# Four small VectorE operations per unit: two of them placed behind the first maximum of a step

## The chip, the core and the metric

The kernel runs on one core of one Trainium2 chip. The metric is the device time of one execution in microseconds (us). A run gives the time of several executions; one further execution is recorded by the hardware profiler, and every row shown below comes from that one.

## What is computed

The reference is one block of a transformer with a gate, for 2048 rows of 512 numbers, all in float32:

```python
xn = _layernorm(x)
# attention, 32 heads of 16, one shared key and value head
q = (xn @ wq) in 32 heads;  k = xn @ wk;  v = xn @ wv
p = softmax(q @ k.T * 16 ** -0.5)
s = (p @ v, heads side by side) @ wo
# two dense layers with Mish between them, then SiLU
h = xn @ w1 + b1
g = silu((h * tanh(softplus(h))) @ w2)
return x + s * g
```

The softmax needs the maximum of every row of scores. The kernel computes the scores twice: once to find the maxima, once (transposed) to take the exponential, with the negated maximum already added inside the matmul.

## The kernel before, in words

**Units and steps.** The queries are cut into 32 units: 4 chunks of 512 rows by 8 groups of 4 heads. A unit takes 16 steps, so there are NS = 512 steps; one step takes about 2.85 us. The loop at L1477 writes out, step by step, the instructions of all engines. Every engine then works through its own list in order and waits only on semaphores. In a usual step stand:

- four score matmuls `m` (L1059) whose results go to three PSUM banks (pool `ps_m`, L130), and behind each one a VectorE maximum over its 512 columns (`top`, L1062 to L1063, tile `mb`). They run 20 steps (LEAD) ahead of the exponentials;
- four score matmuls `e` (L1039) and behind each a ScalarE exponential into `pt` (L1041);
- a share of the dense layers, called filler: matmuls into one PSUM bank `xps` (L118), a group of 9, 12 or 15 at a time, written as two halves of 64 rows each, half by half in two steps. The halves are mixed with the `m` and `e` work by `waves` (L637). Some groups end with a VectorE operation that reads the bank (`y`, L851 or L920), and the next group can start only behind it. To let that operation go early, `waves` holds back the last maxima of such a step (L667, L673);
- at the end of the step the product with the values, `pv` (L1116). Its eight rows per step are a good mark of where TensorE is.

**The four operations.** When all maxima of a unit are there, `c_rows` (L1078) turns them into two rows for each pair of heads. `reduce` (L1085) takes the maximum over the four key blocks; `parts` writes the negated maximum in the reduced matmul format (L1088) and what that format loses (L1090); `turn` (L1095) transposes the result into a tile `cr`, of which there are two; `move` (L1103) issues eight DMAs of 2 KB on SyncE's queue. They put the rows into the query tile `qt`, where the `e` matmuls of the unit read them from the unit's first step on. The four DMAs for the upper half of the partitions are issued first and are needed in that first step, the other four in the next.

**Their place.** At the end of each step the loop checks whether a unit's maxima are complete (L1533). If so, two entries go into `rowq`: `reduce` alone, and `parts`, `turn` and `move` together. One entry is taken at the end of a step unless a filler group with a VectorE ending finished in that step (`evacs`, L1537). Then `pump` (L1540) issues weight loads. Call the step that ends with `reduce` the first, the one that ends with `parts`, `turn` and `move` the second, and the one after it the third. The third step is two or three steps ahead of the unit's first exponential.

**The planner's clocks.** `sp_at` (L147) keeps an estimate of when SyncE's queue is free, in steps; `move` charges it 0.68 us for each DMA. A weight load adds its own charge and derives from the estimate the step from which the loaded tile counts as ready (L469). A filler group begins only in a step in which all its tiles count as ready (`is_ready`, L492); a step without one runs with less on TensorE. Nothing in the running program uses these estimates: a real wait is always a semaphore.

The last units, and what the loop does from step 491 on, have no more maxima to stand behind.

Of the kernel before, what the change touches and what calls it, by code (L numbers as in the profile page):

```python
# [18 lines left out]
AX = mybir.AxisListType  # L19
# [14 lines left out]
LEAD = 20  # L34
# [90 lines left out]
def block_kernel(ctx: ExitStack, tc: tile.TileContext, x, wq, wk, wv, wo, w1, b1, w2, out):  # L125
# [10 lines left out]
    pe, act, dve, pool, sp = nc.tensor, nc.scalar, nc.vector, nc.gpsimd, nc.sync  # L136
# [10 lines left out]
    def sp_at(us):  # L147

        sp_t[0] = max(sp_t[0], step[0] * STEP_US) + us
        return (sp_t[0] + 2.6) / STEP_US - 1  # L150
# [23 lines left out]
    def f(ap):  # L174
        return ap.bitcast(F32)
# [847 lines left out]
    mb_of = {}  # L1023
# [19 lines left out]
        return r  # L1043

    m_next = [0, 0]

    def m_one(a, other=False):
        v, n = MSEQ[m_next[a]] if m_next[a] < 64 else divmod(m_next[a], 32)
        m_next[a] += 1
        if v not in mb_of:  # L1050
            mb_of[v] = sb.tile([P, 4, 16], F32, tag="mb", name=f"mb{v}", bufs=2)
        q = qt_of[v]
        kb, j = divmod(n, 8)
        p, t = divmod(j, 4)
        o = 64 * a
        ps, tag = (ps_e, "e") if other or lead and 15 in xp_of and a else (ps_m, "m")
        m = ps.tile([P, C], F32, tag=tag, name=f"m{v}_{a}_{n}")
        o = slice(o, o + (HALF if v < len(qts) else 48))
        pe.matmul(m, q[o, p, P * t:P * (t + 1)], ks[o, C * kb:C * (kb + 1)], start=True, stop=True)  # L1059
        z = 8 * a + 4 * p + t  # L1060

        def top():  # L1062
            return dve.reduce_max(out=mb_of[v][:, kb, z:z + 1], in_=m, axis=AX.X)  # L1063
        if held[0] is None:
            return top()
        held[0].append(top)
# [11 lines left out]
    def c_rows(v):  # L1078

        mp = sb.tile([P, 2, 3, 8], F32R, tag="mp", name=f"mp{v}", bufs=2)  # L1080
        mx = f(mp[:, :, 0])
        w = {}

        def reduce():
            dve.reduce_max(out=mx, in_=mb_of[v].rearrange("p b (a z) -> p a z b", a=2), axis=AX.X)  # L1085

        def parts():
            dve.tensor_reduce(out=mp[:, :, 1], in_=mx.rearrange("p a (z o) -> p a z o", o=1), axis=AX.X,  # L1088
                              op=ALU.max, negate=True)
            dve.tensor_reduce(out=f(mp[:, :, 2]), in_=f(mp[:, :, 0:2]).rearrange("p a s z -> p a z s"), axis=AX.X,  # L1090
                              op=ALU.add, negate=True)

        def turn():
            cr = w["cr"] = sb.tile([P, 32], F32, tag="cr", name=f"cr{v}", bufs=2)
            dve.transpose(cr, f(mp[:, :, 1:3]).rearrange("p a s z -> p a (s z)"))  # L1095

        def move():
            q, cr = qt_of[v], w["cr"]
            for a in range(1, -1, -1):
                r = 64 * a + 48  # L1100
                for b in range(4):
                    sp_at(0.68)
                    sp.dma_start(f(q[r:r + 2]).rearrange("o p (t b n) -> b o (p t) n", b=4, n=32)[b],  # L1103
                                 cr[32 * b + 16 * a:32 * b + 16 * a + 16])
        return reduce, parts, turn, move

    def pv(s):
        v, k = divmod(s, 16)
# [91 lines left out]
    NS = 16 * NU  # L1200
# [17 lines left out]
    def when(t):  # L1218
        now[0] = t
        step[0] = max(step[0], (t - E0) / STEP_US)  # L1220
        k = min(timed, default=1)
        if k <= step[0] and busy[0] + E0 < t + 0.5 and not plan["POOL"]:
            timed[k].pop(0)()
            if not timed[k]:
                del timed[k]
# [5 lines left out]
    def task(eng, us, fn, deps=(), **kw):  # L1231
        t = Task(eng, us, fn, deps, **kw)
        plan[eng].append(t)
        return t
# [57 lines left out]
    for c0, c1 in ((0, 1), (1, 2), (2, 3), (3, 4)):  # L1292
        z = slice(4 * c0, 4 * c1)
# [63 lines left out]
    def m_ready(t):  # L1357
        if min(m_next) >= 2 * LEAD or rows and rows[-1].end is None:
            return None
        v, n = MSEQ[m_next[0]]  # L1360
        if len(qready.get(v) or ()) <= n % 8 // 4 or n // 8 not in kready:
            return None
        return max(t, qready[v][n % 8 // 4], kready[n // 8], m_ends[-5 if 15 in xp_of else -2])

    def best(eng):
        found = None
        for k in plan[eng]:
            s = k.start(T[eng])
            if s is not None:
                rank = max(s, T[eng] + 0.1) + WAIT_US * k.prio  # L1370
                if found is None or rank < found[2]:
                    found = (s, k, rank)
        return found
# [5 lines left out]
    while True:  # L1379
        opts = []  # L1380
        for e in ("ACT", "DVE", "POOL", "SP"):
            if e == "POOL":
                T[e] = max(T[e], busy[0] + E0)
            if b := best(e):
                early = max(now[0], b[1].start(0))
                opts.append((early if e == "DVE" and b[1].prio < 3 and b[0] < early + 5.0 else b[0], e, b[1]))
        b = best("PE")
        m = m_ready(T["PE"])
        if m is not None and b and b[0] < T["PE"] + 0.2 and T["DVE"] > T["PE"] + 1.0:
            m = None  # L1390
        if m is not None and (b is None or m <= b[0] + 0.05 or T["DVE"] < T["PE"] + 0.3 and m <= T["PE"] + 0.1):
            opts.append((m, "PE", "M"))
        elif b:
            opts.append((b[0], "PE", b[1]))
        e0 = min((o for o in opts if o[1] == "PE"), default=None, key=lambda o: o[0])
        low = min((o[0] for o in opts), default=None)
        if e0 is None or e0[0] > T["PE"] + 0.35:
            opts.append((T["PE"], "PE", "X"))
        if not any(o[1] == "ACT" and o[0] < T["ACT"] + 0.1 for o in opts):
            opts.append((T["ACT"], "ACT", "J"))  # L1400
        s, e, k = min(opts, key=lambda o: o[0])
        if cdone[0] is not None and s >= cdone[0] - 0.4 and min(m_next) >= 2 * LEAD:
            break
        when(s)
        for tag in items:
            load(tag)
        if k == "M":
            if MSEQ[m_next[0]] == (0, 8 * NC - 8):
                keep_warm(3)
            for a in range(2):  # L1410
                m_one(a)
            d = max(T["DVE"], s + 0.45)
            m_ends += [d + 0.6, d + 1.2]
            T["DVE"] = d + 1.2
            T["PE"] = s + (0.25 if kind[0] == "M" else 0.45)
            kind[0] = "M"
            if vdone[0] == 0 and min(m_next) >= m_need(0):
                vdone[0] = 1
                r = c_rows(0)
                r1 = task("DVE", 0.85, lambda r=r: (r[0](), r[1](), r[2]()), prio=-4)  # L1420
                rows[:] = [r1]

                def move():
                    r[3]()
                    cdone[0] = now[0] + 2 * 0.65 + 2.0
                task("SP", 2.6, move, [r1])
        elif k == "X":
            fresh = cur["g"] is None
            if cur["g"] is not None or not waiting and begun[0] < 1 + (s - 18) / X_US and begin():
                begun[0] += fresh  # L1430
                fill(3)
                T["PE"] = s + 0.23 * 3 + (0.2 if kind[0] == "M" else 0)
                kind[0] = "X"
            else:
                keep_warm()
                T["PE"] = s + 0.25
                kind[0] = "X"
        elif k == "J":
            tag = next((g for g in ("wq", "ws", "wb") if (g == "wq" or s > 19.0) and arrived(g) and busy[0] + E0 < s + 0.5), None)
            n = ran[0]  # L1440
            if tag:
                split(tag)
                T["ACT"] = s + 0.6
            else:
                gap[0] = 0
                if not plan["POOL"]:
                    act_jobs(1)
                T["ACT"] = s + (0.65 if ran[0] > n else 0.15)
        else:
            plan[e].remove(k)  # L1450
            k.fn()
            T[e] = max(s, T[e]) + k.us + (0.15 if e == "PE" and kind[0] == "M" else 0)
            k.end = T[e]
            if e == "PE":
                kind[0] = "T"
# [8 lines left out]
    rowq = deque()  # L1464
# [12 lines left out]
    for s in range(NS + 2000):  # L1477
# [54 lines left out]
        step[0] = s  # L1532
        if vdone[0] < 8 * NC and min(m_next) >= m_need(vdone[0]):  # L1533
            r = c_rows(vdone[0])
            rowq.extend([r[0], lambda r=r: (r[1](), r[2](), r[3]())])
            vdone[0] += 1
        if rowq and not evacs[0]:  # L1537
            rowq.popleft()()
        evacs[0] = 0
        pump()  # L1540
        if s > NS + 1 and not queue and cur["g"] is None and not timed and not jobs:
# [13 lines left out]
```

## Time and profile before

| what | value |
|---|---|
| median of 3 runs | 1585.93 us (1585.4 to 1586.27) |
| the profiled execution's own time | 1586.2 us |
| its span, first to last instruction | 1584.4 us |
| mean granted TensorE clock | 0.999 of full speed |
| VectorE busy | 1343.9 us, 85% |
| ScalarE busy | 1306.5 us, 82% |
| GpSimd busy | 626.6 us, 40% |
| DMA | 124.31 MB, mean 78 GB/s |

How to read the rows: in a list of groups a row has the line and engine, the operation, its tiles (out<-in), shapes and count, then busy time, mean length, and the idle time of the engine just before with what ended it. In the timeline a row has the start in us from the span's start, the length in us (of all that it merges, first start to last end), engine, line, operation, tiles and count; in brackets the idle time before it and who ended it. PEld is TensorE's weight load, DVE is VectorE, ACT ScalarE, SPq SyncE's queue and DVEq VectorE's sequencer.

### The profile page before, as it was taken

Reading aid. Unit: us, or ns where it says so; the run is one execution under the profiler, and the core shown is the slowest. Engines: PE = TensorE matmul, PEld = TensorE weight load, DVE = VectorE, ACT = ScalarE, POOL = GpSimd, SP = SyncE. Lnnn points to the kernel's source line nnn. Section 1 sums busy time; section 2 is a strip of 40 time slices with the busy share of each in tenths; the row PEclk is TensorE's granted clock in tenths of the full one; section 3 lists DMA queues with packets and bytes.
Section 4 is the critical chain, followed back from the end, with each engine's and each line's share of the span. In section 5 each row is a group of like instructions: output and inputs, shape, how many; then the busy total and the mean of one; then the engine's idle time right before and its main releaser. Section 6 shows DMA issues by size and latency. Waiting matters only on the chain.

```text
span 1584.4 us, 31651 instructions
## 1 busy us (share of the span) xinstructions
PE 1569.5 (99%) x11717; PEld 840.9 (53%) x11717; DVE 1343.9 (85%) x2341; ACT 1306.5 (82%) x2515; POOL 626.6 (40%) x641
## 2 busy tenths in 40 slices
PE   9999999999999999999999999999999999999998
PEld 5455555555555455555555555555555555555554
DVE  8998888889889888888898988888889998888832
ACT  7488788798898778868988787897898878789886
POOL 3476266284464104513425131362252414225412
PEclk9999999999999999999999999999999999999999
DMA  6233231132331204222122321220332212031011
GB/s 195 94 104 124 65 99 44 52 126 84 125 96 42 101 16 151 58 71 67 38 79 71 98 71 58 84 71 17 123 98 85 68 59 97 17 111 58 15 55 54
DMA packets 74666, 124.31 MB, mean 78 GB/s; under 512 B 21520, under 2 KB 35344, under 8 KB 74512
## 3 DMA queue, kind: packets, MB, share of 16 engines
q1 hardware_dynamic: 74512, 122.29, 24.8%
q8 instruction: 93, 1.52, 0.4%
q14 instruction: 61, 0.50, 0.1%
HBM read 74.78 MB, written 26.21 MB: 64 GB/s over the span
## 4 chain that ended last, share of the span: by engine, by line
PE 95%; DVE 3%; ACT 1%; DMA 1%; issue 0%; SPq 0%; POOL 0%; DVEq 0%; ACTq 0%
PE xps L118 45%; PE pv L1116 32%; PE m L1059 8%; PE e L1039 7%; DVE mb L1063 2%; PE kp L319 1%; ACT pt L1041 1%; DMA wbs<-w 0%; PE xps L114 0%; PE late L118 0%; PE xp L287 0%; PE late L1039 0%; DMA xin<-in_dram 0%; PE wop L114 0%; DVE xt L162 0%
## 5 line engine op out<-in xcount | busy, mean ns | idle before, releaser
L1063 DVE TENSOR_REDUCE mb<-m 128x1 f32<-128x512 f32 x2048 | 1267.9, 681 | 170.1 <-PE m L1059 148.0
L1041 ACT ACTIVATE pt<-e 128x512 f32<-128x512 f32 x2018 | 1061.9, 603 | 224.7 <-PE e L1039 218.7
L1059 PE MATMUL m<-ks,qt 48*128 48x512 f32 (+1 forms) x2048 | 833.1, 422 | 1.8 <-DVE mb L1063 0.9
L1039 PE MATMUL e<-qt,ks 64*128 64x512 f32 x2018 | 744.1, 402 | 0.5 <-ACT pt L1041 0.3
L1116 PE MATMUL pv<-pt,vaug 128*32 128x512 f32 x4096 | 543.1, 604 | 0.0
L1059 PEld LDWEIGHTS m<-ks,qt 48*128 48x128 f32 (+1 forms) x2048 | 372.3, 185 | 67.9 <-DVE mb L1063 32.8
L1039 PEld LDWEIGHTS e<-qt,ks 64*128 64x128 f32 x2018 | 373.3, 186 | 17.0 <-ACT pt L1041 6.6
L118 PE MATMUL xps<-wbs,act 64*128 64x512 f32 x1248 | 338.3, 407 | 1.6 <-DMA wbs<-w 1.1
L118 PEld LDWEIGHTS xps<-wbs,act 64*128 64x128 f32 x1248 | 217.5, 185 | 175.8 <-ACT pt L1041 104.9
L118 PE MATMUL xps<-xt,ws 64*128 64x512 f32 x1104 | 306.1, 410 | 0.9 <-DVE y L851 0.8
L118 PEld LDWEIGHTS xps<-xt,ws 64*128 64x128 f32 x1104 | 190.2, 185 | 183.6 <-ACT pt L1041 121.6
L172 POOL TENSOR_SCALAR t<-t 128x512 f32<-128x512 f32 x56 | 34.4, 615 | 325.1 <-ACT t L784 324.7
L1116 PEld LDWEIGHTS pv<-pt,vaug 128*32 128x32 f32 x4096 | 81.9, 108 | 137.0 <-issue 128.8
L162 POOL TENSOR_TENSOR hb<-hb,t 128x512 f32<-128x512 f32 x56 | 72.2, 1290 | 67.7 <-ACT t L797 46.8
L118 PE MATMUL xps<-xt,wq 64*128 64x512 f32 x336 | 93.2, 410 | 0.0
L118 PEld LDWEIGHTS xps<-xt,wq 64*128 64x128 f32 x336 | 57.9, 185 | 55.0 <-ACT pt L1041 35.2
L118 PE MATMUL xps<-wbs,ot_all 64*128 64x512 f32 x288 | 79.5, 408 | 0.0
L118 PEld LDWEIGHTS xps<-wbs,ot_all 64*128 64x128 f32 x288 | 49.5, 184 | 46.7 <-ACT pt L1041 31.9
L162 POOL TENSOR_TENSOR hb<-hb,u 128x512 f32<-128x512 f32 x56 | 72.3, 1291 | 4.4
L162 POOL TENSOR_TENSOR u<-u,t 128x512 f32<-128x512 f32 x56 | 71.8, 1283 | 4.7
L162 POOL TENSOR_TENSOR act<-hb,act 128x512 fp32r<-128x512 f32 x55 | 70.8, 1287 | 4.6
L162 POOL TENSOR_TENSOR oc<-oc,sc 128x512 f32<-128x512 f32 (+1 forms) x16 | 20.6, 1287 | 118.4 <-ACT sc L1144 47.1
(146 smaller groups left out, 946.5 us busy)
## 6 DMA issues: line engine op xcount, KB each, us to landing
wbs<-w SPq DMA_DIRECT2D x36, 512.0 KB
ws<-w SPq DMA_DIRECT2D x35, 512.0 KB
qt<-qh SPq DMA_DIRECT2D x256, 32.0 KB
wq<-wq SPq DMA_DIRECT2D x14, 512.0 KB
w<-wbs SPq DMA_DIRECT2D x14, 512.0 KB
wbs<-wo SPq DMA_DIRECT2D x12, 512.0 KB
rawws<-in_dram SPq DMA_DIRECT2D x21, 256.0 KB
rawwb<-in_dram SPq DMA_DIRECT2D x20, 256.0 KB
```

The source lines that it names most:

```text
L118: i = self.pe.matmul(ps, self.lhs()[o], self.rhs()[o], start=(self.k == 0 and self.halves == 0), stop=(self.k == self.tot - 1 and self.hal ...
L162: eng.tensor_tensor(out=o, in0=a, in1=b, op=op)
L172: pool.tensor_scalar(o, o, lim, 0.0, op0=ALU.min, op1=ALU.max)
L319: pe.matmul(kp_of[c], wkf[:, dt], xf_of[c][dt // 2][:, dt % 2], start=(dt == 0), stop=(dt == 3))
L1039: pe.matmul(e, ks[o:o + 64, P * k:P * (k + 1)], q[o:o + 64, p], start=True, stop=True)
L1041: r = act.activation(pt, e, AF.Exp, scale=0.25)
L1059: pe.matmul(m, q[o, p, P * t:P * (t + 1)], ks[o, C * kb:C * (kb + 1)], start=True, stop=True)
L1063: return dve.reduce_max(out=mb_of[v][:, kb, z:z + 1], in_=m, axis=AX.X)
L1116: pe.matmul(o[32 * j:32 * j + 32], vaug[:, k], pt, start=(k == 0), stop=(k == 15))
```

## The change

Two functions are made of `parts`: `high` (L1088) and `low` (L1090). A list `behind` is added. Whatever stands first in it is issued directly behind the next maximum that is written out, so behind the first maximum of the following step.

```diff
         def top():
-            return dve.reduce_max(out=mb_of[v][:, kb, z:z + 1], in_=m, axis=AX.X)
+            r = dve.reduce_max(out=mb_of[v][:, kb, z:z + 1], in_=m, axis=AX.X)
+            if behind:
+                behind.popleft()()
+            return r
...
-        def parts():
+        def high():
             dve.tensor_reduce(out=mp[:, :, 1], in_=mx.rearrange("p a (z o) -> p a z o", o=1), axis=AX.X,
                               op=ALU.max, negate=True)
+
+        def low():
             dve.tensor_reduce(out=f(mp[:, :, 2]), in_=f(mp[:, :, 0:2]).rearrange("p a s z -> p a z s"), axis=AX.X,
                               op=ALU.add, negate=True)
...
-            rowq.extend([r[0], lambda r=r: (r[1](), r[2](), r[3]())])
+            rowq.extend([lambda r=r: (r[0](), behind.append(r[1])),
+                         lambda r=r: (r[2](), behind.append(lambda: (r[3](), r[4]())))])
             vdone[0] += 1
         if rowq and not evacs[0]:
             rowq.popleft()()
+        while behind and s >= NS - LEAD - 1:
+            behind.popleft()()
```

So `reduce` stays at the end of the first step, `high` goes behind the first maximum of the second step, `low` stays at the end of the second step, and `turn` and `move` go behind the first maximum of the third step. Unit 0, whose rows are made before the loop, keeps its order, and from step 491 on everything is issued at once.

More of the change, by code (lines that the diff above doesn't have):

```diff
@@ L1045, in block_kernel @@
     m_next = [0, 0]
+    behind = deque()
     def m_one(a, other=False):
@@ L1104, in move @@
                                  cr[32 * b + 16 * a:32 * b + 16 * a + 16])
-        return reduce, parts, turn, move
+        return reduce, high, low, turn, move
     def pv(s):
@@ L1419, in block_kernel @@
                 r = c_rows(0)
-                r1 = task("DVE", 0.85, lambda r=r: (r[0](), r[1](), r[2]()), prio=-4)
+                r1 = task("DVE", 0.85, lambda r=r: (r[0](), r[1](), r[2](), r[3]()), prio=-4)
                 rows[:] = [r1]
                 def move():
-                    r[3]()
+                    r[4]()
                     cdone[0] = now[0] + 2 * 0.65 + 2.0
```

## The prediction

> **What bounds the kernel.** I read the page first (the chain's shares, then the costliest groups), then the chain of waits by stretch, then the timeline of single steps.
>
> ```profile
> PE 95%; DVE 3%; ACT 1%; DMA 1%; issue 0%; SPq 0%; POOL 0%; DVEq 0%; ACTq 0%
> L1063 DVE TENSOR_REDUCE mb<-m 128x1 f32<-128x512 f32 x2048 | 1267.9, 681 | 170.1 <-PE m L1059 148.0
> ```
>
> TensorE is the bound: 95% of the chain. VectorE is behind it in most steps (its maxima wait 148.0 us in all for an `m`). DVE's 3% of the chain is 48 us, but much of that is the lead-in. The chain cut to 90 to 1500 us tells what the loop can give:
>
> ```profile
> by line: PE xps L118 49.5%; PE pv L1116 34.1%; PE m L1059 7.5%; PE e L1039 7.5%; DVE mb L1063 0.5%; DMA wbs<-w 0.5%; ACT pt L1041 0.1%; DVE y L851 0.1%; issue 0.1%; SPq L468 0.0%; SPq L446 0.0%; DVE cr L1095 0.0%; DVEq L1095 0.0%; DVE mp L1
> 542.33 6.84 DMA wbs<-w
> ```
>
> There `mb` has 0.5% of 1410 us, 7 us, and one transfer at 542 us nearly as much. A late maximum also makes TensorE start its next matmul anew, which the chain books on the matmul, so the timeline is needed. Unit 16, VectorE and then TensorE:
>
> ```profile
> 818.01 0.26 DVE L1085 TENSOR_REDUCE mp<-mb 128x16 f32<-128x64 f32 x1
> 818.44 2.48 DVE L1063 TENSOR_REDUCE mb<-m 128x1 f32<-128x512 f32 x4 [0.18 <-PE m L1059]
> 820.84 0.16 DVE L1088 TENSOR_REDUCE mp<-mp 128x16 fp32r<-128x16 f32 x1
> 821.03 0.19 DVE L1090 TENSOR_REDUCE mp<-mp 128x16 f32<-128x32 f32 x1
> 821.44 0.21 DVE L1095 STREAM_TRANSPOSE cr<-mp 128x32 f32<-128x32 f32 x1 [0.21 <-DVE mp L1090]
> 821.57 2.44 DVE L1063 TENSOR_REDUCE mb<-m 128x1 f32<-128x512 f32 x4
> 824.27 0.69 DVE L1063 TENSOR_REDUCE mb<-m 128x1 f32<-128x512 f32 x1 [0.26 <-PE m L1059]
> ```
>
> ```profile
> 816.88 1.07 PE L1116 MATMUL pv<-pt,vaug 128*32 128x512 f32 x8
> 817.88 0.50 PE L1059 MATMUL m<-ks,qt 48*128 48x512 f32 x1
> 819.73 1.06 PE L1116 MATMUL pv<-pt,vaug 128*32 128x512 f32 x8
> 820.72 0.50 PE L1059 MATMUL m<-ks,qt 48*128 48x512 f32 x1
> 822.28 0.49 PE L1059 MATMUL m<-ks,qt 48*128 48x512 f32 x1
> 822.70 1.06 PE L1116 MATMUL pv<-pt,vaug 128*32 128x512 f32 x8
> ```
>
> From `pv` to `pv` the second step takes 2.85 us and the third 2.97. The cause is read off the rows. In the second step the first maximum starts 0.56 us behind its `m` (817.88, 818.44). In the third it could so start at 821.28, but the block from 820.84 on holds it until 821.57: 0.29 us late, ending at about 822.2 (2.44 us for four, less three starts of 0.60). There are three banks for `m`, so the fourth `m` needs the first one's bank: it starts at 822.28, at 0.49 us, the length of a matmul that starts anew.
>
> Is it the block? Unit 1 is the control. Its transposed tile is used for the first time, so nothing is to be waited for ahead of the transpose:
>
> ```profile
> 117.06 0.21 DVE L1095 STREAM_TRANSPOSE cr<-mp 128x32 f32<-128x32 f32 x1
> 115.53 1.07 PE L1116 MATMUL pv<-pt,vaug 128*32 128x512 f32 x8
> 118.38 1.06 PE L1116 MATMUL pv<-pt,vaug 128*32 128x512 f32 x8
> ```
>
> No idle time ahead of the transpose, and the third step takes 2.85 us. So the tolerance lies under 0.29 us, and a block shorter by 0.2 us costs nothing. What the later units wait for stands in the rows of line 1095:
>
> ```profile
> L1095 DVEq EVENT_SEMAPHORE  x120: 49/50/50, 164.0 to 1519.9; - x120
>   DVE mp L1090: 6.9, 29
> ```
>
> Four waits per unit (for the eight DMAs that last read this `cr`) pass through VectorE's sequencer one behind the other; 6.9 us over 29 units, 0.24 us each, is idle engine.
>
> **The change, part by part.** Nothing is removed; the four operations and eight DMAs per unit only move.
>
> *First and second step.* `reduce` stays; it ends at 818.27, ahead of the maximum at 818.44, so it is free now and then. `high` comes behind the second step's first maximum. Independent neighbours overlap: four maxima take 2.48 us, so they start every 0.60 us though one lasts 0.68; `high` (0.16) costs 0.08 us. The four maxima then end at 821.00 instead of 820.92, `low` at about 821.11. That is before 821.28: the third step's first maximum is no longer late. The cover is VectorE's idle time per step, 0.18 to 0.26 us in these rows.
>
> *Third step.* `turn` behind the first maximum. Its four waits run while that maximum computes (0.60 us against 821.03 to 821.44, about 0.4), so the 0.24 us of idle time go too; it costs 0.14 us (821.44 to 821.57) and pushes maxima two to four. Their banks are needed in the next step, where VectorE idled 0.26 us, so nothing is late. If the cover is gone (the waits run only behind the maximum), it costs 0.4 us more, of which the idle 0.26 takes most.
>
> So each third step like that of unit 16 falls from 2.97 to 2.85. The same marks in all units give 23 such steps (unit 3, 5 to 10, 12, 14 to 18, 20 to 29) at 0.12 to 0.14 us; first and last:
>
> ```profile
> 210.00 1.06 PE L1116 MATMUL pv<-pt,vaug 128*32 128x512 f32 x8
> 212.98 1.06 PE L1116 MATMUL pv<-pt,vaug 128*32 128x512 f32 x8
> 1425.65 1.06 PE L1116 MATMUL pv<-pt,vaug 128*32 128x512 f32 x8
> 1428.63 1.06 PE L1116 MATMUL pv<-pt,vaug 128*32 128x512 f32 x8
> ```
>
> **Term one: 23 x 0.13 = 3.0 us.**
>
> In units 13 and 30 the third step ends a filler group whose `y` the block delays, and the next group waits for the bank:
>
> ```profile
> 681.66 0.16 DVE L1088 TENSOR_REDUCE mp<-mp 128x16 fp32r<-128x16 f32 x1
> 682.39 1.25 DVE L1063 TENSOR_REDUCE mb<-m 128x1 f32<-128x512 f32 x2
> 684.29 0.49 PE L118 MATMUL xps<-wbs,act 64*128 64x512 f32 x1 [0.40 <-DVE y L851]
> 1477.03 0.49 PE L118 MATMUL xps<-xt,ws 64*128 64x512 f32 x1 [0.76 <-DVE y L851]
> ```
>
> There the block takes 0.73 us (681.66 to 682.39). After, 0.08 + 0.11 + 0.14 = 0.33 us stand ahead of `y`, so it comes 0.40 us sooner: the first gap closes. Unit 30's is longer because its transpose idled 0.56 us; I take 0.6 of 0.76, since what it waited for may still be late. Four more units (9, 11, 15, 17) show 0.1 us of the same kind; I take 0.3 in all. **Term two: 0.4 + 0.6 + 0.3 = 1.3 us**, bounds 0 and 1.6.
>
> *SyncE's queue.* The eight DMAs stay in front of what is issued at the end of the third step, but what `pump` issues at the end of the second and what is due at the start of the third now stands ahead of them. By the program's order that is nothing in most units, and a load and a store in unit 10:
>
> ```profile
> 535.56 5.32 SPq L1103 DMA_DIRECT2D qt<-cr  x8
> 540.98 0.35 SPq L468 DMA_DIRECT2D wbs<-w  x1
> 541.43 0.38 SPq L446 DMA_DIRECT2D w<-wbs  x1
> 541.90 0.38 SPq L468 DMA_DIRECT2D wq<-wq  x1
> 542.33 1.29 SPq L468 DMA_DIRECT2D wbs<-w  x1
> 549.21 0.50 PE L118 MATMUL xps<-wbs,act 64*128 64x512 f32 x1 [1.08 <-DMA wbs<-w]
> ```
>
> Held up behind the row DMAs, four transfers of 512 KB run together, and TensorE waits 1.08 us for the last, which took 6.84 us. After, the first two are out of the way before the row DMAs, and two run together: about half of 6.84 us, and 549.2 becomes 546 to 547, ahead of the need at 548.1. **Term three: 1.1 us**, bounds 0 and 1.1. The planner books `move` one step later, which makes loads of the third step count as ready up to a step later. For unit 10's group the last tile then counts as ready exactly in the step in which the group began; I expect no group to begin later. A missed step would move a quarter of a group, 3 matmuls of 0.23 us, to the end: 0.7 us.
>
> *The rows themselves.* `turn` starts at 821.28 + 0.60 = 821.88 instead of 821.44: 0.44 us later, and TensorE comes 0.13 sooner. Unit 11 bounds how long a row DMA takes, for its `e` did not wait:
>
> ```profile
> 591.15 1.26 SPq L1103 DMA_DIRECT2D qt<-cr  x2
> 593.81 0.19 PEld L1039 LDWEIGHTS e<-qt,ks 64*128 64x128 f32 x1
> 823.11 1.26 SPq L1103 DMA_DIRECT2D qt<-cr  x2
> 826.66 0.19 PEld L1039 LDWEIGHTS e<-qt,ks 64*128 64x128 f32 x1
> ```
>
> The fourth DMA (second of the row) was issued at about 591.8, so it lands in at most 2.0 us. In unit 16 it was issued at about 823.75 and needed at 826.66: at least 0.9 us to spare, against 0.57 used up. Unit 11 itself may wait a little: 0 to 0.3 us, taken as 0.
>
> One page speaks against part of this. The Trainium skill, "VectorE: DVE Perf Modes", section "The DRAIN you can't avoid", says that a next operation starts only when the pipe is empty and that a semaphore between chained operations costs nothing extra. By it nothing overlaps, and an operation costs its full length anywhere. The trace has four maxima of 0.68 us in 2.48 us; the rows differ, and they decide. By the page `low` would still end at 821.27, and only term two would shrink, by some 0.2 us.
>
> **Sum:** 3.0 + 1.3 + 1.1 = 5.4 us. The profiled execution took 1586.2 us, 1.8 of it outside its span; it stands 0.3 us above the median. 1586.2 - 5.4 = 1580.8, against the median 1580.5. I take **1580.6 us**.
>
> **Rivals.**
> *Half of it (0.14).* Only term one comes: other transfers take the place of the one at 542 us, and the `y` stay late. For it: these are single events. 1586.0 - 3.0 = 1583.0, or 1582 with part of term two.
> *No change (0.06).* The third step is late for another reason, or the lateness passes to the fourth. Against it: unit 1, and the slack of 0.26 us. 1586.
> *Slower: the rows come late (0.10).* At a unit's first step its `e` wait for the row DMAs. Place: the border of every unit. It begins to cost when the eight DMAs start over 0.9 us later than now rather than 0.44; each us beyond costs 30 us, and the gain is gone at 0.2 us beyond. A load ahead of the row DMAs, or a first maximum that comes late, could do it in single units; for all units `turn` would have to slip behind the second maximum (0.60 more, 1.04 + 0.13 in all): 30 x 0.27 = 8 us lost against 5.4 won, 1588.5.
> *Forecast (0.70).*
>
> **The numbers.** A measurement of this kernel can tell about 0.2% (3.2 us) from no change. Faster: 0.70 and half of the first rival, a little off for what the trace can't show, 0.75. Same: the rest of it, no change and a mild form of the slow case, 0.15. Slower: 0.10. The range runs from 1578.6 (all terms at their upper bounds, 5.7, and 1.5 for what I missed) to 1584.5 (term one half won).
>
> **What would show it.** Right: third steps at 2.85 in the units named; no idle time ahead of L1095; no gap on `y` at units 13 and 30; no wait for `wbs` near 549 us. Wrong: an `e` that waits for `qt`, or a fourth step of 2.97.

## The result and the profile after

The changed kernel takes 1580.58 us (median of 6 runs, 1580.12 to 1581.24), the kernel before 1586.18 us beside it (1585.4 to 1586.61). The ratio is 0.9964, 95% interval 0.9954 to 0.9975: faster by 0.36%, 5.6 us. The profiled span fell from 1584.4 to 1578.7 us.

In the listing of the changed kernel the lines of `m`, its maximum, `reduce`, `high`, `low`, `turn`, `move` and `pv` are 1060, 1064, 1089, 1092, 1096, 1101, 1109 and 1122.

From the page after, the shares of the chain; behind it the chain cut to 90 to 1500 us:

```profile
PE 96%; DVE 2%; ACT 1%; DMA 0%; SPq 0%; issue 0%; POOL 0%; ACTq 0%; DVEq 0%
```

```profile
by line: PE xps L118 48.6%; PE pv L1122 34.6%; PE e L1039 8.8%; PE m L1060 7.7%; DVE mb L1064 0.1%; ACT pt L1041 0.1%; issue 0.1%; ACT y L845 0.0%
```

The maxima have gone from 0.5% to 0.1% of that stretch, and the transfer of `wbs` is out of it. Unit 16 again, VectorE in the timeline after:

```profile
814.70 0.26 DVE L1089 TENSOR_REDUCE mp<-mb 128x16 f32<-128x64 f32 x1
815.15 0.69 DVE L1064 TENSOR_REDUCE mb<-m 128x1 f32<-128x512 f32 x1 [0.19 <-PE m L1060]
815.76 0.16 DVE L1092 TENSOR_REDUCE mp<-mp 128x16 fp32r<-128x16 f32 x1
815.84 1.88 DVE L1064 TENSOR_REDUCE mb<-m 128x1 f32<-128x512 f32 x3
817.63 0.18 DVE L1096 TENSOR_REDUCE mp<-mp 128x16 f32<-128x32 f32 x1
818.00 0.69 DVE L1064 TENSOR_REDUCE mb<-m 128x1 f32<-128x512 f32 x1 [0.19 <-PE m L1060]
818.61 0.20 DVE L1101 STREAM_TRANSPOSE cr<-mp 128x32 f32<-128x32 f32 x1
818.73 1.84 DVE L1064 TENSOR_REDUCE mb<-m 128x1 f32<-128x512 f32 x3
```

The third step's first maximum (818.00) now waits 0.19 us for its matmul instead of being late itself, and nothing stands idle ahead of the transpose. `high` costs 0.08 us (815.76 to 815.84), `turn` 0.12 (818.61 to 818.73). TensorE's `pv` marks around the third step of units 3, 16 and 29:

```profile
209.71 1.06 PE L1122 MATMUL pv<-pt,vaug 128*32 128x512 f32 x8
212.56 1.07 PE L1122 MATMUL pv<-pt,vaug 128*32 128x512 f32 x8
...
816.44 1.07 PE L1122 MATMUL pv<-pt,vaug 128*32 128x512 f32 x8
819.28 1.06 PE L1122 MATMUL pv<-pt,vaug 128*32 128x512 f32 x8
...
1420.90 1.07 PE L1122 MATMUL pv<-pt,vaug 128*32 128x512 f32 x8
1423.76 1.06 PE L1122 MATMUL pv<-pt,vaug 128*32 128x512 f32 x8
```

They are 2.85, 2.84 and 2.86 us apart; before, in units 3, 16 and 29, it was 2.97 to 2.98. SyncE's queue in unit 10, and the step of TensorE that had waited for the transfer:

```profile
526.41 0.87 SPq L468 DMA_DIRECT2D wbs<-w  x2
527.92 0.32 SPq L446 DMA_DIRECT2D w<-wbs  x1
534.90 5.32 SPq L1109 DMA_DIRECT2D qt<-cr  x8
540.33 0.34 SPq L468 DMA_DIRECT2D wq<-wq  x1
540.71 0.43 SPq L468 DMA_DIRECT2D wbs<-w  x1
```

```profile
544.65 1.07 PE L1122 MATMUL pv<-pt,vaug 128*32 128x512 f32 x8
547.83 1.06 PE L1122 MATMUL pv<-pt,vaug 128*32 128x512 f32 x8
```

One load and one store have moved from behind the row DMAs to 7.0 to 8.5 us ahead of them (526.41 is two loads, one of them new there). The step takes 3.18 us; before it took 4.44 (545.90 to 550.34) with the wait in it.

Where the 5.7 us of the span went, by the `pv` marks of all steps: third steps -2.97, fourth steps -1.25, the one step at 544 us -1.26, and -0.33 ahead of the first `pv`. That last part can't be put down to the change: the first `pv` of the ten profiles in this study lies anywhere between 86.7 and 87.6 us. All other steps together are longer by about 0.1 us.

### The profile page after: what moved, and what is told of

Same layout as the page of the kernel before. It is cut to its first block, busy times and chain, and to the rows that moved or that the text cites. A ratio compares the mean times of both kernels' runs of the same rounds, so it can differ in the third digit from the quotient of the medians.

```text
span 1578.7 us, 31652 instructions
## 1 busy us (share of the span) xinstructions
PE 1566.1 (99%) x11717; PEld 842.6 (53%) x11717; DVE 1341.9 (85%) x2341; ACT 1306.6 (83%) x2515; POOL 626.4 (40%) x641
## 4 chain that ended last, share of the span: by engine, by line
PE 96%; DVE 2%; ACT 1%; DMA 0%; SPq 0%; issue 0%; POOL 0%; ACTq 0%; DVEq 0%
PE xps L118 44%; PE pv L1122 32%; PE e L1039 8%; PE m L1060 8%; DVE mb L1064 2%; PE kp L319 1%; PE xps L114 0%; ACT pt L1041 0%; PE xp L287 0%; PE late L118 0%; DMA xin<-in_dram 0%; PE late L1039 0%; PE wop L114 0%; DVE xt L162 0%; SPq L224 0%
```

## The experiments

Theory: only the lateness of the third step's first maximum counts; the block at the end of the second step (`high`, `low` and `turn` on VectorE) made it late, largely by the waits ahead of the transpose. Rivals: each operation taken out of the block is worth its own length; the order of the transfers makes the gain; the rows come late. Each kernel was timed beside the kernel before; the intervals of the faster ones overlap, and those of e3 and e4 include no change at all. So the steps of one profile of each kernel decide, the third steps by 23 repeats, the single steps by one. In the table "third steps" is the mean over the 23 units of the prediction, "behind 13, 30" the fourth steps of those units, "9, 15, 17" the mean of theirs.

| kernel | us | ratio to before | third steps | behind 13, 30 | 9, 15, 17 | step at 544 us |
|---|---|---|---|---|---|---|
| before | 1586.18 | | 2.98 | 3.54, 3.69 | 2.99 | 4.44 |
| changed | 1580.58 | 0.9964 (0.9954 to 0.9975) | 2.85 | 3.11, 2.91 | 2.97 | 3.18 |
| e1_turn_only | 1580.93 | 0.9965 (0.9952 to 0.9978) | 2.85 | 3.23, 3.11 | 2.97 | 3.19 |
| e2_high_only | 1581.89 | 0.9971 (0.9961 to 0.9982) | 2.85 | 3.23, 3.04 | 2.88 | 3.92 |
| e3_cr14 | 1584.86 | 0.9994 (0.9984 to 1.0003) | see below | 3.36, 3.34 | 2.98 | 4.10 |
| e4_move_only | 1585.47 | 0.9995 (0.9986 to 1.0004) | 2.98 | 3.54, 3.70 | 2.99 | 3.20 |
| e5_second_max | 1581.06 | 0.9965 (0.9952 to 0.9978) | 2.85 | 3.11, 2.92 | 2.97 | 3.19 |
| e6_fourth_max | 1611.32 | 1.0157 (1.0142 to 1.0172) | 2.85 | 3.06, 2.86 | 2.98 | 3.49 |
| e8_high_first | 1580.77 | 0.9965 (0.9952 to 0.9977) | 2.85 | 3.16, 2.96 | 2.88 | 3.18 |
| e9_high_move | 1580.77 | 0.9966 (0.9953 to 0.9979) | 2.85 | 3.23, 3.05 | 2.88 | 3.18 |

### The waits taken away, nothing moved (e3_cr14)

```diff
-            cr = w["cr"] = sb.tile([P, 32], F32, tag="cr", name=f"cr{v}", bufs=2)
+            cr = w["cr"] = sb.tile([P, 32], F32, tag="cr", name=f"cr{v}", bufs=14)
```

This is an edit of the kernel before.

> The kernel before the change with 14 transposed tiles instead of two, nothing moved. Up to unit 13 the transpose then has no earlier DMAs to wait for; from unit 14 on it has, so the run holds its own control. Theory (the four waits make the block long enough to be late): third steps of 2.85 in units 3, 5 to 10 and 12, of 2.97 in units 14 to 18 and 20 to 29; the gap on y at unit 13 about 0.2 us shorter, at unit 30 as before, the wait near 549 us as before. 1586.2 less 8 x 0.13 and 0.2 is 1585.0 us. Rival (the number of operations between two steps counts, not the waits): 2.97 in all units and 1586.2 us.

The run holds its own control. The rows of `cr`, then `pv` around the third step of unit 12 (no waits) and of unit 16 (waits):

```profile
  DVE mp L1090: 4.2, 18
```

```profile
631.91 1.06 PE L1116 MATMUL pv<-pt,vaug 128*32 128x512 f32 x8
634.75 1.07 PE L1116 MATMUL pv<-pt,vaug 128*32 128x512 f32 x8
...
818.75 1.07 PE L1116 MATMUL pv<-pt,vaug 128*32 128x512 f32 x8
821.73 0.64 PE L1116 MATMUL pv<-pt,vaug 128*32 128x512 f32 x4
```

All eight units without waits have 2.84 to 2.85 us, though `high`, `low` and `turn` stand in one block as before; those from 14 on have 2.97 to 2.99 (unit 22 has 3.34, see below). In the eight the first maximum is 0.10 to 0.12 us late, with no cost. So it is the waits that made the block too long, as the theory said; the rival that counts operations is out. The fourth step behind unit 13 fell by 0.18 us (0.2 expected).

Two steps were not expected to change: the fourth step behind unit 30 is 0.35 us shorter, and the third step of unit 22 is 0.37 longer than in the kernel before. Both hang on the idle time ahead of the transpose. First unit 30 before the change, then units 22 and 30 in e3:

```profile
1474.99 0.21 DVE L1095 STREAM_TRANSPOSE cr<-mp 128x32 f32<-128x32 f32 x1 [0.56 <-DVE mp L1090]
```

```profile
1101.82 0.21 DVE L1095 STREAM_TRANSPOSE cr<-mp 128x32 f32<-128x32 f32 x1 [0.58 <-DVE mp L1090]
1474.02 0.21 DVE L1095 STREAM_TRANSPOSE cr<-mp 128x32 f32<-128x32 f32 x1 [0.21 <-DVE mp L1090]
```

An extra 0.35 us stood ahead of unit 30's transpose (and unit 11's) and stands at unit 22's in e3. Count VectorE's instructions in the trace, its sequencer's included, from 0: the one that comes late is number 959 and 2367 before and number 1727 in e3, so they lie multiples of 128 apart, and an 8192-byte packet on the instruction queue q14 begins 0.6 to 0.7 us after each. With 48 waits fewer in its program, e3 has another unit's block at such a place. That instructions are loaded there is likely but was not tested.

### The order of the transfers alone (e4_move_only)

```diff
-            rowq.extend([lambda r=r: (r[0](), behind.append(r[1])),
-                         lambda r=r: (r[2](), behind.append(lambda: (r[3](), r[4]())))])
+            rowq.extend([r[0], lambda r=r: (r[1](), r[2](), r[3](), behind.append(r[4]))])
```

This and all that follow are edits of the changed kernel.

> The four VectorE operations stand where they stood before the change; only the eight row DMAs are issued later, in the third step behind its first maximum, so what was issued behind them at the end of the second step now stands ahead of them. Theory (the third term alone): third steps of 2.97 as before, gaps on y at units 13 and 30 as before, no wait for wbs near 549 us; 1586.2 less 1.2 is 1585.0 us. Rival (the order of the transfers makes the gain): near 1580.6 us. Rival (the wait at 542 to 549 us went for another reason): 1586.2 us with the wait still there.

TensorE around the place of the wait:

```profile
546.38 1.06 PE L1122 MATMUL pv<-pt,vaug 128*32 128x512 f32 x8
549.58 1.06 PE L1122 MATMUL pv<-pt,vaug 128*32 128x512 f32 x8
```

The step takes 3.20 us, 1.24 less than before, and no other step differs by 0.06 us. So the order gives the third term and only that. Where the old order was kept, the step took 4.44, 3.92 and 4.10 us: the wait is always there, its length is not steady.

### One half of the spreading, then the other (e1_turn_only, e2_high_only)

From here on the diffs show the lines put in; those that they replace are the second line of the changed kernel's two, and in e1 and e8 both.

```diff
 # e1_turn_only
+            rowq.extend([r[0], lambda r=r: (r[1](), r[2](), behind.append(lambda: (r[3](), r[4]())))])
 # e2_high_only
             rowq.extend([lambda r=r: (r[0](), behind.append(r[1])),
+                         lambda r=r: (r[2](), r[3](), r[4]())])
```

> The changed kernel, but the two short reductions stay together at the end of the second step; only the transpose and the row DMAs stand behind the first maximum of the third step. Theory (only the lateness of the third step's first maximum counts): the two reductions end about 0.38 us after the last maximum has started its tail, still before 0.56 us behind the third step's first score matmul, so no third step is late: 2.85 us in all 23 units, the gap on y at units 13 and 30 stays closed, the wait near 549 us stays away, and the time is that of the changed kernel, 1580.6 us, within 0.7. Rival (every operation moved out of the block is worth its own length): high is a third of the block, so a third of the first term is lost, third steps of about 2.89 us and 1581.6 us.

> The changed kernel, but only the first short reduction stands behind a maximum; the second one, the transpose and the row DMAs are at the end of the second step as before the change. Theory: the block is 0.11 us shorter than before, so the third step's first maximum is 0.18 us late instead of 0.29. Unit 1 before (0.11 late) cost nothing and a fourth step of the changed kernel that is 0.24 late costs 0.12 us, so this lies between: third steps of 2.85 if the tolerance is over 0.18, 2.93 to 2.98 if it is under. The gaps on y at units 13 and 30 come back at about 0.3 and 0.65 us, and the wait for wbs near 549 us comes back, since the row DMAs stand in front of the loads again. 1582.0 to 1585.5 us. Rival (each operation is worth its own length): third steps of 2.93. Rival (the order of the transfers makes the gain): 1586.

Either half alone brings all third steps to 2.85. The rival that pays each operation by its length is out: the two gains don't add, they are both the whole of it. But the theory missed in e2: it had the first maximum 0.18 us late, and it isn't late at all. VectorE in e2 in the second and third step of unit 16, then the rows of the transpose's line in that stretch (the four waits, first and last start):

```profile
817.20 1.87 DVE L1064 TENSOR_REDUCE mb<-m 128x1 f32<-128x512 f32 x3
818.99 0.18 DVE L1096 TENSOR_REDUCE mp<-mp 128x16 f32<-128x32 f32 x1
819.20 0.21 DVE L1101 STREAM_TRANSPOSE cr<-mp 128x32 f32<-128x32 f32 x1
819.35 1.89 DVE L1064 TENSOR_REDUCE mb<-m 128x1 f32<-128x512 f32 x3
```

```profile
L1101 DVEq EVENT_SEMAPHORE  x4: 50/50/50, 817.9 to 818.2; - x4
```

The same row for unit 16 before the change:

```profile
L1095 DVEq EVENT_SEMAPHORE  x4: 49/50/50, 821.0 to 821.3; - x4
```

Before, the waits begin when `low` begins (821.03). In e2 the last of them begins 0.8 us before `low` does (818.2, 818.99): VectorE's sequencer has run ahead of its engine by two instructions. What differs is only that `high` no longer stands directly in front of `low`, so that `low` has nothing to wait for.

### The gain without `behind` on VectorE (e8_high_first, e9_high_move)

```diff
 # e8_high_first
+            rowq.extend([lambda r=r: (r[0](), r[1]()), lambda r=r: (r[2](), r[3](), behind.append(r[4]))])
 # e9_high_move
             rowq.extend([lambda r=r: (r[0](), behind.append(r[1])),
+                         lambda r=r: (r[2](), r[3](), behind.append(r[4]))])
```

> Nothing stands behind a maximum on VectorE: the first short reduction goes to the end of the first step, directly behind reduce; the second one and the transpose stay at the end of the second step; the row DMAs are issued in the third step behind its first maximum. Theory (in the block of before, the second reduction waits for the first one just in front of it, holds VectorE's sequencer by that and lets the transpose's four waits begin only when it starts; separated, the sequencer runs ahead and the four waits pass under the last maximum): the four waits stand ahead of the last maximum's start, no 0.21 us of idle time ahead of the transpose, third steps of 2.85 in all 23 units, second steps of 2.85 too since reduce and high end about 0.02 us late, fourth steps of units 9, 15 and 17 of 2.89 instead of 2.97, no wait near 549 us: 1580.4 us, within 0.7. Rival (the four waits always run behind the second reduction): 0.2 us idle ahead of the transpose, the third step's first maximum 0.18 us late, third steps of 2.85 to 2.93 and 1580.6 to 1582.5 us.

> As the kernel in which only the first short reduction stood behind a maximum (second reduction and transpose at the end of the second step), but with the row DMAs issued in the third step behind its first maximum. Theory (the parts that gain, taken together): third steps of 2.85 in all 23 units, fourth steps of units 9, 15 and 17 of 2.89 as there, steps behind units 13 and 30 of 3.23 and 3.04 as there, and no wait near 549 us, which that kernel still had (1.0 us): 1581.9 less 0.7 to 1.0 is about 1581.0 us, and against the changed kernel 0.3 us won at units 9, 15 and 17 and 0.25 lost at 13 and 30, so the same as it within what can be measured. Rival (the two parts interfere): third steps over 2.85 or the wait back, 1582 us or more.

e8 tests the reading of e2 in another arrangement: `high` one step earlier, `low` and `turn` where they always were. VectorE in unit 16, then the waits:

```profile
814.66 0.26 DVE L1089 TENSOR_REDUCE mp<-mb 128x16 f32<-128x64 f32 x1
814.95 0.17 DVE L1092 TENSOR_REDUCE mp<-mp 128x16 fp32r<-128x16 f32 x1
815.11 2.48 DVE L1064 TENSOR_REDUCE mb<-m 128x1 f32<-128x512 f32 x4
817.51 0.17 DVE L1096 TENSOR_REDUCE mp<-mp 128x16 f32<-128x32 f32 x1
817.72 0.21 DVE L1101 STREAM_TRANSPOSE cr<-mp 128x32 f32<-128x32 f32 x1
817.96 1.29 DVE L1064 TENSOR_REDUCE mb<-m 128x1 f32<-128x512 f32 x2
```

```profile
L1101 DVEq EVENT_SEMAPHORE  x4: 50/50/50, 816.5 to 816.8; - x4
```

The waits pass 0.7 us ahead of `low`, and the transpose follows it at once. `low` and `turn` are still next to each other, and this costs nothing. e8 and e9 are as fast as the changed kernel. By their steps they gain 0.1 us at each of units 9, 15 and 17 and lose 0.05 to 0.14 behind units 13 and 30; no run beats the change by more than can be measured.

### How late the rows may come (e5_second_max, e6_fourth_max)

```diff
 # the two edits in one line: n is 1 in e5_second_max, 3 in e6_fourth_max
+                         lambda r=r: (r[2](), behind.extend([lambda: None] * n + [lambda: (r[3](), r[4]())]))])
```

> The changed kernel with the transpose and the row DMAs behind the second maximum of the third step instead of the first: 0.60 us later. This measures how much time the rows have left. Only the 22 units whose third step is two steps ahead of their first exponential (5, 7, 11 to 30) can be late; the others have 2.85 us more. Theory (at least 0.33 us of the 0.9 are left, what is missing is paid once per unit): between no loss, 1580.6 us, and 22 x 0.27 = 6 us, 1586.6 us, with waits of the first e of a unit for the row DMAs of 0 to 0.27 us; I take 0.1 and 1582.5. Rival (the rows were never near their limit): 1580.6 us.

> The changed kernel with the transpose and the row DMAs behind the fourth maximum of the third step: 1.8 us later than behind the first. Theory (the slower rival of the prediction, with its price): each of the 22 units whose third step is two steps ahead of the first exponential waits 1.8 us less what is left, 0.33 to 0.9 us, so 0.9 to 1.5 us each, 20 to 33 us in all: 1600 to 1614 us, and waits of e for the DMAs into qt in the chain. The other units wait for nothing. Rival (rows this late are still in time): 1580.6 us.

0.60 us later costs nothing; 1.8 us later (2.4 to 2.7 in units 11, 13, 15, 17, 19 and 30) costs 30.7 us against the changed kernel. From the list of waits and from the chain (90 to 1500 us) of e6:

```profile
PE e L1039 <- DMA qt<-cr: 16.3, 19, 1.7
PEld e L1039 <- DMA qt<-cr: 7.0, 6, 2.0
```

```profile
739.16 1.66 DMA qt<-cr
1072.75 1.66 DMA qt<-cr
1168.73 1.66 DMA qt<-cr
```

The loss falls on the border of the 22 units, whose steps are longer by 0.85 to 2.4 us, by 1.0 to 1.1 in eleven of them. So some 0.75 us were left after the change (1.8 less 1.05; by the units with the least loss up to 0.95), and the chain has 1.66 us from the issue of the row DMA that was waited for to its landing.

## Why the prediction was right

- **The bound and the cause.** Right. The block made the third step's first maximum late; unit 1 was a fair control, and e3 made eight more like it among the 23.
- **Term one, 3.0 us.** 2.97 measured. The mechanism is as told, but more was moved than was needed: e1 and e2 each give all of it. What the prediction did not see is why the four waits cost anything. It took them as a fixed price that a maximum must cover. They cost 0.21 us only because `low` stood behind the operation that it waits for; e2 and e8 hide them with the transpose left in its place.
- **The tolerance.** It was put under 0.29 us. 0.11 us late (e3) costs nothing, and 0.29 costs 0.13. In the fourth step of unit 17, 0.24 (the changed kernel) costs 0.09 more than 0.15 (e8). Whether 0.15 is free isn't shown: that step takes 2.88 us there, and no run has it on time.
- **Term two, 1.3 us.** 1.25 measured, by other shares: 0.43 behind unit 13 (0.4 foretold), 0.78 behind unit 30 (0.6), and 0.04 in all from units 9, 11, 15 and 17 instead of 0.3. In unit 30 the prediction left open what the transpose had waited for beyond the usual. It was the extra 0.35 us, which moved with the program in e3. In the changed kernel the four waits of unit 30 are still spread out (1469.0 to 1469.7), but under a maximum, so all of the gap went. In units 9, 15 and 17 `turn` behind the first maximum stands ahead of the VectorE operation that ends the group, and the next step's first maximum is still 0.24 us late; with `turn` back in the second step (e8) it is 0.15 late and the step is 2.88 instead of 2.97. The prediction had counted that 0.14 us ahead of `y` for units 13 and 30 and left it out for these. Its sign of being wrong, a fourth step of 2.97, is met in units 9, 15 and 17, but no lateness was passed on there: those steps had 2.99 before.
- **Term three, 1.1 us.** 1.26 measured, 1.24 by e4 alone: the mechanism is right, the size a little above the bound of 1.1. The last load was issued at 540.71 instead of 542.33 and was in time. The size is in part luck of the profile before: against the waits of e2 and e3 the same order would have won 0.7 and 0.9 us.
- **The rows.** The 0.57 us used up are right in size. The bound of 0.9 us that it was set against was too careful: 0.57 plus 0.75 makes 1.3. The point from which the slower rival decides was therefore wrong. It gave 1588.5 us for a transpose behind the second maximum, and e5 has 1581.06. Its place holds: e6 pays at the border of the unit. Its price of 30 us for each us was put on 30 units; 22 pay, since the others have a whole step more.
- **The page.** The Trainium skill, "VectorE: DVE Perf Modes", section "The DRAIN you can't avoid", reports eight copies that take 13.88 us with a semaphore behind each of them as with one behind the last, and says that the semaphore costs nothing extra there. Here `low` directly behind `high`, whose result it needs, starts 0.19 us after it (821.03 against 820.84), while a maximum that needs nothing of it starts 0.08 after it (815.84 against 815.76). For this kernel the measurement decides: about 0.11 us, and with it the sequencer is held. The prediction read the section as if nothing could overlap, and that was too strict: the section also says that a next operation that is not held starts earlier. The four maxima of 0.68 us in 2.48 us agree with that.
- **The sum, 5.4 us.** The three terms measure 5.48, the other steps take 0.1 of it back, and 0.33 in the lead-in came by chance. That the forecast of 1580.6 us meets the median of 1580.58 so closely is therefore in part luck, since term two was too small at one unit and too large at four others, and term three was too small.

## What to carry to other kernels

Ask of a small operation on an almost full engine not what it costs but which bank, and whose next start, it delays: here 0.11 us late was free and 0.24 was not, and half of the change (e1) would have given all but 0.3 us of the gain in the loop. Keep an operation that needs the result of the one just before it away from that place, above all when waits on other engines or DMAs follow it. And look at what an in-order DMA queue holds up: moving eight small DMAs by a fraction of a step was worth 1.2 us, because two large transfers went ahead of them.

## What was not expected of the hardware

In unit 16 of e8 VectorE's sequencer began the four waits 1.0 us ahead of the operation in front of the transpose (816.5 against 817.51), past a maximum that had not begun. It ran ahead in this way in e2, e8 and e9, where no instruction ahead had to wait, and not where `low` waited for `high`. In the changed kernel the waits of unit 16 begin with the maximum in front of the transpose, which had itself waited 0.19 us for its matmul (818.00):

```profile
L1101 DVEq EVENT_SEMAPHORE  x4: 50/50/50, 818.0 to 818.3; - x4
```

That a waiting instruction holds the sequencer is the reading of these rows; how many instructions it may run ahead at most was not tried. What sets the places of the extra 0.35 us, seen at three transposes, was not tried either.
